# The scores of a batch's last 64 columns: four down matmuls behind the second score group, or right behind it

## Chip, cores and metric

One core of one Trainium2 chip. The metric is the device time of one execution in microseconds. Most executions of a kernel agree within 0.3%; now and then one is slower at a lower granted clock. A run more than 1.5% above the kernel's fastest counts as slow and is left out of the ratios; a milder one stays in, and is named where it matters. In all texts "position n" is the n-th of the 64 matmuls of one down stage, "the rest" is the last 64 token columns of a batch, and "a switch" is the change of PE between scores (64-row tiles) and matmuls over 128 rows. In the profile's lines PE is the matmul engine and PEld its weight loads, ACT is ScalarE, DVE is VectorE, and "<-" names what ended an idle time.

## The reference

Attention over keys and values that are averaged in groups of eight, then an up projection, `h * cos(h)`, and a down projection:

```python
k_p = k.reshape(B, H, Sp, pool, D).mean(axis=3)        # B, H, S, D = 8, 8, 576, 64; pool = 8, Sp = 72
v_p = v.reshape(B, H, Sp, pool, D).mean(axis=3)
scores = scale * np.matmul(q, k_p.transpose(0, 1, 3, 2))
attn = np.exp(scores - max); attn = attn / sum(attn)   # cut
x = np.matmul(attn, v_p) ...                           # 4608 tokens x 512
h = x @ w_in                                           # 512 -> 2048
out = (h * np.cos(h)) @ w_out                          # 2048 -> 512
```

## The kernel before

The tokens are worked in nine tiles of 512. A tile's up matmul (64 matmuls, `up_mm`) is followed by its down matmul (64, `down_mm`). A batch has 576 tokens, so tiles and batches drift apart. In tiles 1 to 6 the down matmul of tile t carries, as `fill`, the attention of batch b = t + 1: four units of 256 columns x 4 heads (`us[0]` to `us[3]`), and the rest of batch t (`REST`, 64 columns x 8 heads). A unit is scores on PE, an exp on ScalarE, values on PE, two logs and an inverse on ScalarE, two multiplies on VectorE into `xT`. All of this goes through three PSUM tiles of two banks each, called bank 0 to 2; two more single banks hold the down sums.

```python
banks = [psum.tile([128, 2, 512], FP32, name=f"bank{i}") for i in range(3)]
obanks = [psum.tile([128, 512], FP32, name=f"obank{i}") for i in range(2)]
...
def values(b, u, pair, later=None):
    ...   # matmuls into pair, two logs (L247), one inverse exp (L248) on ScalarE
    def mul():
        for hp in range(2):
            nc.vector.tensor_mul(out=x_out(b, u, half[hp]), in0=cols(pair[half[hp], hp, :], u),   # L252
                                 in1=cols(inv[half[1 - hp]], u))
...
fill = [(4, two_(0, 2, 0)), (14, V_(0, 1)), (19, V_(1, 2)), (32, two_(2, 0, 1)), (36, fill[0][1]),
        (38, V_(2, 0)), (41, V_(3, 1)), (45, fill[1][1])]
for n, (ms, fc) in enumerate(mms):
    while fi < len(fill) and fill[fi][0] <= n:
        fill[fi][1]()
        fi += 1
    down_mm(obanks[ms % 2], ms, fc)
    if fc == FFCH - 1:
        down_out(t, ms, obanks[ms % 2])
```

`V_(1, 2)` at 19 puts the values of unit 1 into bank 2. The two groups `two_` at 4 and 32 are scores of two units and then both exps. `fill[0][1]` at 36 is the rest's scores and exp, again in bank 2.

The softmax here doesn't subtract the row's maximum and nothing guards it: scores larger than these inputs give would overflow.

## Time and profile before

| | before |
|---|---|
| median of the first runs | 303.87 us |
| PE busy | 294.0 of 302.1 us |
| one steady stage (up and down of one tile) | 31.41 us |
| steady stages that the change touches | 6 |

PE is the bound: a stage is the sum of what PE has in its list, plus what PE waits. The stage length is read from one load of the cosine table to the next on ScalarE, at 115.21 and 146.62 us. The lines that carry the argument are in the prediction.

### The profile page before, as it was taken

To read this page: it belongs to the slowest core of one execution; us is meant where nothing else is said; L and a number is where in the kernel's file an instruction comes from. 1 tells how busy PE (TensorE), PEld (TensorE's weight loads), DVE (VectorE), ACT (ScalarE), POOL (GpSimd) and SP (SyncE) were. 2 spreads that over 40 slices of the span, in tenths; PEclk is the share of its full clock that TensorE was granted. 3 is DMA by queue.
4 is the path that set the end of the run, shared out by engine and by line. 5 is a ranking of instruction groups with operands and counts; after the bars stand their busy time and mean duration, and the time that the engine had idled before them with its cause. 6 is when DMAs were issued, how large, how long until landed. Compare 5 with 4: busy or idle time off the path is not lost.

```text
span 302.1 us, 4605 instructions
## 1 busy us (share of the span) xinstructions
PE 294.0 (97%) x1798; PEld 141.6 (47%) x1798; DVE 172.3 (57%) x211; ACT 206.8 (68%) x255; POOL 129.8 (43%) x92
## 2 busy tenths in 40 slices
PE   8799999999999999999999999999999999999995
PEld 3545544445544454455444544454444544444444
DVE  5558636574566366645675566656574567425712
ACT  3887897469856986688768876788578956606500
POOL 8553007984973596349733991399100000000000
PEclk9999999999999999999999999999999999999999
DMA  7999999639546943695169617881900330131032
GB/s 152 201 207 206 208 204 196 152 44 174 109 113 105 167 92 70 123 171 113 44 132 161 115 36 162 129 141 36 167 5 1 71 69 0 27 79 35 0 71 71
DMA packets 44006, 32.92 MB, mean 109 GB/s; under 512 B 22096, under 2 KB 39248, under 8 KB 43984
## 3 DMA queue, kind: packets, MB, share of 16 engines
q0 software_dynamic: 19744, 18.07, 38.2%
q1 hardware_dynamic: 24080, 14.42, 21.0%
q8 instruction: 14, 0.23, 0.3%
q10 hardware_dynamic: 160, 0.13, 0.2%
q14 instruction: 8, 0.07, 0.1%
HBM read 36.70 MB, written 9.44 MB: 153 GB/s over the span
## 4 chain that ended last, share of the span: by engine, by line
PE 85%; DMA 10%; POOL 2%; ACT 1%; issue 0%; DVE 0%; POOLq 0%; ACTq 0%
PE obank L310 39%; PE bank L297 37%; DMA w_out_sb<-in_moe_w_out_dram 6%; PE bank L241 5%; DMA w_in_sb<-in_moe_w_in_dram 4%; PE bank L211 3%; PE bank L328 1%; POOL kv_st L84 1%; POOL kp L384 1%; POOL q_b L84 1%; ACT L285 0%; ACT cos L304 0%; ACT ex L218 0%; POOL identity masks.py:197 0%; DVE o_sb L316 0%
## 5 line engine op out<-in xcount | busy, mean ns | idle before, releaser
L310 PE MATMUL obank<-w_out_sb,g_sb 128*128 128x512 bf16 x560 | 132.5, 380 | 0.5 <-DMA w_out_sb<-in_moe_w_out_dram 0.5
L297 PE MATMUL bank<-xT,w_in_sb 128*128 128x512 bf16 x576 | 126.5, 379 | 0.0
L304 ACT ACTIVATE cos<-bank,half_pi 128x1024 f32<-128x1024 f32 x72 | 80.0, 1113 | 63.3 <-PE bank L297 63.3
L307 DVE TENSOR_TENSOR g_sb<-bank,cos 128x1024 bf16<-128x1024 f32 x72 | 88.1, 1225 | 48.2 <-ACT cos L304 48.2
L297 PEld LDWEIGHTS <-w_in_sb 128*128 128x128 bf16 x576 | 55.5, 98 | 68.6 <-DVE xT L252 2.5
L310 PEld LDWEIGHTS <-g_sb 128*128 128x128 bf16 x560 | 52.2, 97 | 56.9 <-issue 3.7
L252 DVE TENSOR_TENSOR xT<-bank,inv 64x512 bf16<-64x512 f32 (+1 forms) x72 | 45.3, 629 | 50.1 <-ACT inv L248 49.2
L141 POOL TENSOR_TENSOR kv_st<-kv_st 72x2048 f32<-72x2048 bf16 x12 | 48.7, 4056 | 35.2 <-DMA kv_st<-in_k_dram 35.2
L247 ACT ACTIVATE lnc<-bank 64x512 f32<-64x512 f32 (+1 forms) x72 | 39.2, 544 | 2.9 <-PE bank L241 1.3
L218 ACT ACTIVATE ex<-bank 72x1024 bf16<-72x1024 f32 (+1 forms) x40 | 35.0, 928 | 5.3 <-PE bank L211 5.2
L316 DVE COPY o_sb<-obank 128x512 f32<-128x512 f32 x35 | 23.6, 689 | 16.8 <-PE obank L310 16.2
L142 POOL TENSOR_TENSOR kv_st<-kv_st 72x1024 f32<-72x1024 f32 x12 | 28.2, 2348 | 1.0
L248 ACT ACTIVATE inv<-lnc 128x512 f32<-128x512 f32 (+1 forms) x36 | 21.0, 583 | 1.1
L241 PE MATMUL bank<-ex,vz 72*128 72x256 bf16 (+1 forms) x176 | 20.0, 243 | 0.2 <-ACT ex L218 0.2
L241 PEld LDWEIGHTS <-vz 72*128 72x128 bf16 x176 | 13.7, 97 | 9.9 <-issue 0.6
L145 POOL TENSOR_TENSOR kp<-kv_st 72x512 bf16<-72x512 f32 x12 | 14.9, 1264 | 0.5
L211 PE MATMUL bank<-qT,kk 64*72 64x256 bf16 (+1 forms) x192 | 13.3, 252 | 1.1 <-ACT qT L193 0.5
L211 PEld LDWEIGHTS <-kk 64*72 64x72 bf16 x192 | 7.6, 110 | 11.9 <-issue 8.1
L285 ACT ACT_TABLE_LOAD x9 | 11.5, 1283 | 0.9 <-PEq L515 0.7
L288 ACT ACT_TABLE_LOAD x9 | 11.5, 1283 | 0.2
L495 POOL COPY gate<-kk 1x1 bf16<-1x1 bf16 x5 | 0.9, 180 | 24.7 <-DMA kk<-kp 24.7
L84 POOL DMA_DIRECT2D q_b<-in_q_dram x10 | 7.7, 773 | 2.7 <-DMA w_in_sb<-in_moe_w_in_dram 1.4
(55 smaller groups left out, 89.8 us busy)
## 6 DMA issues: line engine op xcount, KB each, us to landing
out_dram<-o_sb SPq DMA_DIRECT2D x70, 128.0 KB, 2.4
kv_st<-in_v_dram POOLq DMA_DIRECT2D x8, 576.0 KB, 13.0
kv_st<-in_k_dram POOLq DMA_DIRECT2D x7, 576.0 KB, 7.7
q_b<-in_q_dram POOLq DMA_DIRECT2D x6, 576.0 KB, 9.9
w_in_sb<-in_moe_w_in_dram POOLq DMA_DIRECT2D x4, 512.0 KB, 13.7
w_out_sb<-in_moe_w_out_dram POOLq DMA_DIRECT2D x4, 512.0 KB, 18.4
q_b<-in_q_dram POOLq DMA_DIRECT2D x4, 288.0 KB, 12.1
g_sb<-in_k_dram SPq DMA_DIRECT2D x1, 576.0 KB, 3.5
```

What stands on the lines that cost most here:

```text
L141: add(out=s, in0=x[:, :, 0:4, :], in1=x[:, :, 4:8, :], op=ADD)
L142: add(out=s[:, :, 0:2, :], in0=s[:, :, 0:2, :], in1=s[:, :, 2:4, :], op=ADD)
L211: nc.tensor.matmul(pair[:Sp, bank, c:c + n].rearrange("p (g n) -> p g n", n=64), lhsT=kk[b % 2][half[r], h0 + i, 0:Sp], rhs=att["qT", b][h ...
L218: nc.scalar.activation(out=ex[:, 0:nh * n].rearrange("p (a n) -> p a n", a=2), in_=pair[:Sp, :, 0:nh * n // 2], func=ACTF.Exp, scale=scale ...
L241: nc.tensor.matmul(pair[:, hp, (i // 2) * n:(i // 2 + 1) * n], lhsT=vz[b % 2][:, pj, 2 * hp:2 * hp + 2, :].rearrange("p a d -> p (a d)"), ...
L247: nc.scalar.activation(out=lnc[half[1 - hp]], in_=pair[half[1 - hp], hp, 0:w], func=ACTF.Ln)
L252: nc.vector.tensor_mul(out=x_out(b, u, half[hp]), in0=cols(pair[half[hp], hp, :], u), in1=cols(inv[half[1 - hp]], u))
L297: nc.tensor.matmul(h[:, j, :], lhsT=w_in_sb[fc // 4][:, ki, (fc % 4) * 128:(fc % 4 + 1) * 128], rhs=xT[:, ki, t * TILE:(t + 1) * TILE], st ...
L304: nc.scalar.activation(out=cos, in_=h, func=ACTF.Sin, bias=half_pi[:, :1])
L307: nc.vector.tensor_mul(out=g_sb[:, 2 * fp:2 * fp + 2, :], in0=h, in1=cos)
L310: nc.tensor.matmul(o, lhsT=g_sb[:, fc, ms * 128:(ms + 1) * 128], rhs=w_out_sb[fc // 4][:, fc % 4, :], start=(fc == 0), stop=(fc == FFCH - 1))
L316: nc.vector.tensor_copy(out=o[:, 0:n], in_=ps)
```

## The change

Its intent: the scores of the rest follow the second group's directly, so that PE switches once from down matmuls to scores and back where it switched twice; all three exps are written behind all the scores.

```diff
-            def two_(n, bank0, bank1):
+            def scores_of(*parts):
                 def go():
-                    for mm in (scores_mm, scores_exp):
-                        mm(b, us[n], banks[bank0])
-                        mm(b, us[n + 1], banks[bank1])
+                    for f in scores_mm, scores_exp:
+                        for b_, u, bank in parts:
+                            f(b_, u, banks[bank])
                 return go
-            fill = [(4, two_(0, 2, 0)), (14, V_(0, 1)), (19, V_(1, 2)), (32, two_(2, 0, 1)), (36, fill[0][1]),
+            fill = [(4, scores_of((b, us[0], 2), (b, us[1], 0))), (14, V_(0, 1)), (19, V_(1, 2)),
+                    (32, scores_of((b, us[2], 0), (b, us[3], 1), (t, REST, 2))),
                     (38, V_(2, 0)), (41, V_(3, 1)), (45, fill[1][1])]
```

## The prediction

> **What bounds the kernel now.** I read the engine totals first, then the chain that ended last, then the instructions of one steady down stage in order of time. The kernel alternates an up matmul (64 matmuls a tile) and a down matmul (64 a tile) over nine tiles; in tiles 1 to 6 the down matmul also carries the attention of the next batch, as "fill". The change touches only those six stages.
>
> Engine totals of the page (busy us, share of the span, instructions):
>
> ```profile
> PE 294.0 (97%) x1798; PEld 141.6 (47%) x1798; DVE 172.3 (57%) x211; ACT 206.8 (68%) x255; POOL 129.8 (43%) x92
> ```
>
> PE has no idle time to speak of, so whatever lengthens PE's own sequence lengthens the span. The chain that ended last says the same for a steady stage. It is merged, its columns being start us, length us, engine, tile, line, count (L310 is the down matmul, L297 the up matmul, L211 the scores, L241 the values):
>
> ```profile
> 135.95 2.81 PE obank L310 x13
> 138.76 0.56 PE bank L211 x8
> 139.31 0.97 PE obank L310 x4
> 140.28 0.26 PE bank L211 x8
> 140.54 0.54 PE obank L310 x2
> 141.07 0.44 PE bank L241 x4
> ...
> 143.70 4.10 PE obank L310 x19
> 147.80 13.90 PE bank L297 x64
> ```
>
> 13 down matmuls in 2.81 us are 0.216 us each: that is the price of one. The eight scores at 138.76 are the second score group (units 2 and 3), the eight at 140.28 are those of the batch's last 64 columns ("the rest"), and four down matmuls stand between. Exactly these four are what the change moves behind the rest.
>
> Now the same stretch with the other engines, from the timeline (start us, length us, engine, line, operation; in brackets the idle time before it and what ended it; a piece's length includes the modelled tail of its last matmul):
>
> ```profile
> 137.82 0.63 ACT L248 ACTIVATE inv<-lnc 128x512 f32<-128x512 f32 x1
> 138.02 0.69 DVE L316 COPY o_sb<-obank 128x512 f32<-128x512 f32 x1
> 138.69 0.63 PE L211 MATMUL bank<-qT,kk 64*72 64x256 bf16 x8
> 138.75 1.39 DVE L252 TENSOR_TENSOR xT<-bank,inv 64x512 bf16<-64x512 f32 x2
> 139.14 2.41 ACT L218 ACTIVATE ex<-bank 72x1024 bf16<-72x1024 f32 x3 [0.68 <-PE bank L211]
> 139.25 1.04 PE L310 MATMUL obank<-w_out_sb,g_sb 128*128 128x512 bf16 x4
> 140.21 0.21 PEld L211 LDWEIGHTS <-kk 64*72 64x72 bf16 x8 [0.42 <-DVE xT L252]
> 140.21 0.33 PE L211 MATMUL bank<-qT,kk 64*72 64x64 bf16 x8
> 140.91 0.60 PE L241 MATMUL bank<-ex,vz 72*128 72x256 bf16 x4
> 141.61 1.19 ACT L247 ACTIVATE lnc<-bank 64x512 f32<-64x512 f32 x2
> 147.72 12.20 PEld L297 LDWEIGHTS <-w_in_sb 128*128 128x128 bf16 x58 [0.41 <-DVE xT L252]
> ```
>
> The reader is to see one coincidence. The rest's scores go into bank 2. Bank 2 was last used by the values of unit 1 (position 19 of the down matmul), and VectorE's two multiplies out of it (L252) run from 138.75 to 138.75 + 1.39 = 140.14. The rest starts at 140.21, that is 0.07 us after bank 2 came free. The other five stages show the same: multiplies from 76 to 234 us of the span end 0.07 to 0.08 us before the rest's weight loads start. So position 36 was just late enough. The four down matmuls before it cover the time in which bank 2 is still being read.
>
> How quick can PE be after such a release? Tile 0 has a place where PE really was held by the same multiplies (46.42 + 1.39 = 47.81, weights at 47.86):
>
> ```profile
> 46.42 1.39 DVE L252 TENSOR_TENSOR xT<-bank,inv 64x512 bf16<-64x512 f32 x2
> 47.86 0.33 PEld L241 LDWEIGHTS <-vz 72*128 72x128 bf16 x4 [0.53 <-DVE xT L252]
> ```
>
> So 0.05 us, and the 0.07 of the steady stage leaves at most 0.02 to win.
>
> **What the Trainium skill says.** "TensorE: Matmul & The Clock Gate", section "Step-by-step: what each phase is for": matmuls stay in program order, and only weight loads are pulled ahead. So a score that waits for bank 2 holds every down matmul behind it; the trace agrees as far as it goes (the held values of tile 0 let nothing pass). The same page, "Back-to-back issue gap", gives about 216 ns for an isolated 512-column gap and 131 ns as sustained; the trace has 2.81/13 = 216 ns in a sustained stream, and I use that. "PSUM — Partial Sum Buffer", section "PSUM bank collisions raise a hardware error", says that a bank that two engines touch is not arbitrated, so software has to order them; that is the wait the rest carries, and it cannot be dropped. "Perfetto Trace Analysis", section "Tensor Engine Instruction (MATMUL, LD_WEIGHTS)", says that a matmul's reported start is its prefetch and its end an estimate; hence the tenth of a microsecond of slack in my sums.
>
> **The change part by part.** The instruction order confirms what the diff suggests. On PE, in each of the six stages, four down matmuls move from before the rest's eight scores to after them; nothing is added or removed. ScalarE's and VectorE's orders do not change at all: ScalarE ran the three exps in that same order already. "All their exps behind both" is therefore only the order in the program text.
>
> - Taken away: one switch from scores back to down matmuls. Ten down matmuls after the first score group take 2.26 us in the chain, 0.10 above 10 x 0.216, and the four here take 0.97, 0.11 above 0.864. So a switch costs about 0.1 us, up to 0.6 us for six stages, if nothing else is in the way.
> - Added: a hold. After the eight scores PE is ready for the rest at about 139.25. Bank 2 comes free at 140.14 + 0.05 = 140.19. When VectorE gets there depends on nothing that moves: last up matmul, the cos, the table load, two exps, the logs and inverses on ScalarE up to 138.45, with an output copy (138.02 to 138.71) just ahead on VectorE. PE therefore idles about 0.94 us, where it ran four down matmuls before.
> - Moved: those four, 4 x 0.216 = 0.864 us, now run after the rest. The rest starts at 140.19 in place of 140.21. Before, values of unit 2 started 0.70 us after the rest began (eight scores, two downs); now 0.70 + 0.864. They go from 140.91 to about 140.19 + 1.56 = 141.75, +0.84.
> - Does it carry to the end of the stage? ScalarE's logs started at 141.61, directly behind the exps (139.14 + 2.41 = 141.55) and behind the values. Now they wait for the values, about 142.45. From there ScalarE and then VectorE run without gaps until the multiply that the next up matmul waits for (147.72), so this shifts by the same 0.84, and so do PE's own 19 last down matmuls. PE also saves a little by starting the rest on an empty array: the down matmul's modelled tail, 139.25 + 1.04 = 140.29, reached 0.08 past the rest's start. That may give back up to 0.08 a stage.
>
> Sum: 0.76 to 0.86 us a stage, I take 0.82; times 6 is 4.9 us. On 303.87: 308.8 us, +1.6%.
>
> **The rivals.**
>
> - The switch is saved and no hold appears: 303.87 - 0.6 = about 303.3. For it speaks the intent, and that PE's weight loads were idle 0.42 us before the rest exactly as before the other score groups, where the profile names no releaser but issue, so the rest may not have been held before. Against it: no hold before says nothing of 0.9 us earlier, when the multiplies have run for only half a microsecond.
> - The hold is there but is absorbed, because ScalarE or VectorE was the bound of the second half of the stage and has slack to give. The up matmul's first weights waited for VectorE (0.41 us idle at 147.72), and steady up stages take 13.90 us where the one behind tile 0 takes 13.81, so the attention chain is level with PE, not behind it. At most 0.09 a stage comes back if the chain should move less than PE: 308.3.
> - The exps come later too: if the first exp had to wait for the rest's scores, it would start at about 140.5 in place of 139.14, the logs behind the third exp at 142.9 and not 142.45, and another 0.45 us a stage would be lost: 311.5, +2.5%. Against it: the two exps have their own matmuls to wait for, the list of waits on ScalarE is the same in both kernels, and only the third exp reads bank 2.
> - A slow restart after each idle, 0.1 to 0.2 us: 309.4 to 310.0. Nothing in tile 0's held values shows one.
>
> **Range and chances.** The floor is firm: the rest cannot be written before 140.14, so four matmuls less 0.07 and less the 0.08 tail remain, 0.71 a stage, 308.1. The ceiling of the plain mechanism is 0.86 and some latency, 309.3; a slow restart adds half a microsecond. I give 308.0 to 309.8. Two per cent is 309.95, so slower by more needs the restart or the late exps: 0.09. Faster by 2% would need 6 us that no step offers: 0.01. Within 2%: 0.90.
>
> **What would show it.** In the changed profile the rest's scores should begin about 0.05 us after the end of L252, with PE idle 0.8 to 0.95 us before them (5 us in all, put down to VectorE's xT), PE busy time unchanged or a little lower, and a stage of about 32.2 us where it was 31.4. The six down matmuls after the rest should take about 1.3 to 1.4 us, the exps should start as long after the second score group as before, and ScalarE should be idle about 0.8 us before the logs. I am wrong if L252 ends earlier in the stage than now, if the stage does not stretch although the hold is there, or if the first exp starts only after the rest.

## The result

| | before | after |
|---|---|---|
| median | 303.81 us (4 runs, 303.62 to 308.21) | 308.81 us (4 runs, 308.65 to 309.09) |
| PE busy | 294.0 us | 293.9 us |
| one steady stage | 31.41 us | 148.88 - 116.62 = 32.26 us |

The changed kernel is slower by a ratio of 1.0168, 95% interval 1.0148 to 1.0188: clear of noise, and inside 2%. Ratios here are the mean time of one kernel's fast runs over that of the other's of the same rounds, so not quite the ratio of the medians quoted. PE does the same work in the same busy time; the 5 us are waiting. Six stages of 0.85 us are 5.1 us, close to the 5.0 between the medians.

The chain that ended last in the changed kernel, over one steady stage (start us, length us, what), to be laid beside the chain of the kernel before:

```profile
140.17 0.36 PE bank L211 x4
140.53 0.02 issue
140.55 1.03 ACT ex L218
141.58 0.03 issue
141.61 0.33 PE bank L211 x8
141.94 1.40 PE obank L310 x6
143.34 0.44 PE bank L241 x4
...
145.96 4.10 PE obank L310 x19
150.06 13.91 PE bank L297 x64
```

The chain now leaves PE in mid-stage and comes back 1.08 us later. It goes through ScalarE's exp, and not through VectorE as forecast. The timeline of the same stage shows why one should not take that at its word:

```profile
138.02 1.20 ACT L247 ACTIVATE lnc<-bank 64x512 f32<-64x512 f32 x2
...
140.10 0.63 PE L211 MATMUL bank<-qT,kk 64*72 64x256 bf16 x8
140.16 1.39 DVE L252 TENSOR_TENSOR xT<-bank,inv 64x512 bf16<-64x512 f32 x2
140.55 2.41 ACT L218 ACTIVATE ex<-bank 72x1024 bf16<-72x1024 f32 x3 [0.68 <-PE bank L211]
141.61 0.21 PEld L211 LDWEIGHTS <-kk 64*72 64x72 bf16 x8 [1.14 <-DVE xT L252]
141.61 0.33 PE L211 MATMUL bank<-qT,kk 64*72 64x64 bf16 x8 [0.88 <-ACT ex L218]
143.17 0.60 PE L241 MATMUL bank<-ex,vz 72*128 72x256 bf16 x4
143.87 1.19 ACT L247 ACTIVATE lnc<-bank 64x512 f32<-64x512 f32 x2 [0.91 <-PE bank L241]
```

VectorE's multiplies end at 140.16 + 1.39 = 141.55, ScalarE's first exp of the group at 141.58, and the rest starts at 141.61. The weight load is put down to VectorE, the matmul to ScalarE. Both releases lie within 0.03 us, and the profile names the last. By what the program needs, the exp has nothing to do with the rest's scores: it reads bank 0. But a wait can be laid wider than the need, so this had to be tested.

The list of waits (us in total, times, longest), first of the kernel before, then of the changed one:

```profile
PEld L211 <- DVE xT L252: 3.0, 7, 0.4
```

```profile
PEld L211 <- DVE xT L252: 7.3, 7, 1.1
PE bank L211 <- ACT ex L218: 5.3, 6, 0.9
```

The last line is the loss: six idles of PE, 5.3 us, which the kernel before does not have.

### The profile page after: what moved, and what is told of

The parts are those of the page before. It is cut to its first block, busy times and chain, and to the rows that moved or that the text cites. A ratio compares the mean times of both kernels' runs of the same rounds, so it can differ in the third digit from the quotient of the medians.

```text
span 306.9 us, 4605 instructions
## 1 busy us (share of the span) xinstructions
PE 293.9 (96%) x1798; PEld 142.3 (46%) x1798; DVE 172.4 (56%) x211; ACT 206.8 (67%) x255; POOL 129.8 (42%) x92
## 4 chain that ended last, share of the span: by engine, by line
PE 83%; DMA 9%; ACT 3%; POOL 2%; issue 1%; DVE 0%; POOLq 0%; ACTq 0%
PE obank L310 39%; PE bank L297 36%; DMA w_out_sb<-in_moe_w_out_dram 6%; PE bank L241 5%; DMA w_in_sb<-in_moe_w_in_dram 3%; PE bank L211 3%; ACT ex L218 2%; PE bank L328 1%; POOL kv_st L84 1%; POOL kp L384 1%; POOL q_b L84 1%; ACT L285 0%; ACT cos L304 0%; POOL identity masks.py:197 0%; DVE o_sb L316 0%
```

## The experiments

Theory 1 is the prediction's: the rest's scores wait for VectorE's multiplies of unit 1 out of bank 2. Theory 2 is what the chain of the changed kernel shows: they wait for ScalarE's first exp. The first four runs shared a chip, the last two another one. One of the seven runs of the kernel before on the first chip took 307.08 us at a clock of 0.989 and still counts as fast; without it the ratios of these four runs would be about 0.0015 higher. Two of the runs below hold such a run of their own; there the medians and the steady stages say more than the ratio.

Two things could be settled without a run. A kernel that puts the two exps of the second group in the text before the rest's scores, all at position 32, builds into the same instructions with the same waits on all five engines as the changed kernel (but for the numbering of the exps' buffers). "All their exps behind both" changes nothing; the position of the rest's scores is the whole change. And the built program of the changed kernel says what the rest waits for: its first weight load waits for unit 1's second multiply on VectorE, its first matmul for unit 1's second log on ScalarE, both of which read bank 2. That log had ended at 138.02 + 1.20 = 139.22 us; no exp is in either wait. The runs have to say whether the time follows this.

**The output copy first on VectorE, in the changed kernel.** The multiplies of unit 0 are emitted two positions later, behind the copy of the first 128 output rows, which then runs in time that VectorE had idle.

```diff
-            fill = [..., (14, V_(0, 1)), (19, V_(1, 2)),
+            fill = [..., (14, V_(0, 1, later)), (16, lambda: later.pop()()), (19, V_(1, 2)),
```

> The changed kernel with VectorE's order turned: the output copy of the first 128 rows goes ahead of both units' multiplies, so the multiplies of unit 1 can start when their inverse is ready (138.45 in the profile before) and not behind the copy (138.75). Theory 1, VectorE's multiplies hold the rest's scores: bank 2 comes free about 0.28 us earlier in each of six stages, so 308.8 - 1.7 = 307.1 us, and PE's idle before the rest falls from 0.9 to about 0.6 us. Theory 2, the hold is ScalarE's first exp of the second group (the releaser that the profile after names for the matmul, it ends within 0.03 us of the multiplies): nothing on ScalarE moves, so 308.8 us as the changed kernel.

Measured: 307.66 us median (307.35 to 307.87), ratio to before 1.0108 (1.0054 to 1.0162), correct. Timeline of this kernel:

```profile
139.91 1.39 DVE L252 TENSOR_TENSOR xT<-bank,inv 64x512 bf16<-64x512 f32 x2 [0.50 <-ACT inv L248]
140.10 0.63 PE L211 MATMUL bank<-qT,kk 64*72 64x256 bf16 x8
140.56 2.42 ACT L218 ACTIVATE ex<-bank 72x1024 bf16<-72x1024 f32 x3 [0.67 <-PE bank L211]
141.36 0.33 PE L211 MATMUL bank<-qT,kk 64*72 64x64 bf16 x8 [0.63 <-DVE xT L252]
```

In both profiles the second score group starts at 140.10, so they can be laid over each other. The multiplies moved from 140.16 to 139.91, and the rest from 141.61 to 141.36: both by 0.25 us. The rest again starts 0.06 us behind the multiplies (139.91 + 1.39 = 141.30), and the profile now names VectorE. Theory 2 wanted no change; here the rest even starts before the first exp has ended (140.56 and the 1.03 us that it has in the chain of the changed kernel, 141.59). Per stage the gain is 32.26 - 32.01 = 0.25 us, 1.5 us in six, a little under the 0.28 expected. The medians show 1.13 us, taken against the kernel with the group at 29 below (308.79 us on the same chip, as slow as the changed kernel); the difference to 1.5 is of the size of the spread of the runs and is left open.

**The same turn in the kernel before, as control.** The edit is the same, made in the list before.

> The same turn of VectorE's order in the kernel before, as control. Theory 1: there the four down matmuls cover the multiplies anyway, so nothing: 303.8 us within 0.3. If the turn alone is worth time in any kernel (a shorter VectorE chain), it would be about 1.7 us here too: 302.1.

Measured: 304.06 us median (303.95 to 307.66), ratio 1.0019 (0.9943 to 1.0095), correct. The profiled run was the one of 307.66: its clock was 0.91 in the first 60 us, so nothing is read from there; its steady stage is 150.21 - 118.80 = 31.41 us, exactly that of the kernel before, although the multiplies start 0.19 us before the second score group there (142.09 and 142.28) and not 0.06 behind it. So bank 2 a quarter of a microsecond earlier is worth nothing where four down matmuls cover it, and is worth time only where PE stands waiting.

**The rest at 34.**

```diff
-                    (32, scores_of((b, us[2], 0), (b, us[3], 1), (t, REST, 2))),
+                    (32, scores_of((b, us[2], 0), (b, us[3], 1))), (34, scores_of((t, REST, 2))),
```

> The rest's scores two down matmuls behind the second group, halfway between the two kernels. Theory 1, the rest is pinned to the release of bank 2 and each down matmul ahead of it is covered: halfway, 308.8 - 6 x 2 x 0.216 = 306.2 us. If the loss were that of two neighbouring score groups of different batches (a step, not a slope), it would be gone at once: 303.8.

Measured: 306.16 us median (305.88 to 310.81, the last slow), ratio 1.0059 (0.9977 to 1.0142), correct. The steady stage is 147.40 - 115.57 = 31.83 us, halfway between 31.41 and 32.26. The loss is a slope: each down matmul taken from in front of the rest costs its own 0.216 us a stage, since the rest stays tied to the multiplies: in that profile it starts at 140.56 us, 0.06 behind their end (139.11 + 1.39).

**The second group at 29, the rest left at 32.**

```diff
-                    (32, scores_of((b, us[2], 0), (b, us[3], 1), (t, REST, 2))),
+                    (29, scores_of((b, us[2], 0), (b, us[3], 1))), (32, scores_of((t, REST, 2))),
```

> The changed kernel with the second group's scores and exps three down matmuls earlier (29), the rest left at 32. Theory 1, VectorE's multiplies hold the rest: they do not move, so the rest still starts about 0.05 us after them and the time stays, 308.5 to 309.0 us. Theory 2, ScalarE's first exp of the second group holds it: that exp starts about 0.65 us earlier, so the rest does too, and about 3.9 us come back: 304.9.

Measured: 308.79 us median (308.52 to 309.01), ratio 1.0145 (1.0092 to 1.0199), correct. Timeline of this kernel:

```profile
140.26 2.66 ACT L218 ACTIVATE ex<-bank 72x1024 bf16<-72x1024 f32 x3
140.52 1.39 DVE L252 TENSOR_TENSOR xT<-bank,inv 64x512 bf16<-64x512 f32 x2
141.97 0.33 PE L211 MATMUL bank<-qT,kk 64*72 64x64 bf16 x8 [0.77 <-DVE xT L252]
```

The exps now start before the multiplies, the first ends some 0.7 us before the rest starts (140.26 and the 1.03 that it has in the chain of the changed kernel), and still the rest waits, 0.06 us behind the multiplies' end at 141.91. The stage is 149.24 - 116.98 = 32.26 us. Theory 2 falls: moving the exp by itself moves nothing, and moving the multiplies moves the rest.

**All three at 36.** The join without the hold, to see whether the saved switch is there at all.

```diff
-                    (32, scores_of((b, us[2], 0), (b, us[3], 1), (t, REST, 2))),
+                    (36, scores_of((b, us[2], 0), (b, us[3], 1), (t, REST, 2))),
```

> All three groups of scores together, but at position 36, where bank 2 is free: the join without the hold. If PE's own sequence were all that counts: one switch of 0.1 us a stage saved, 303.8 - 0.6 = 303.2 us. My theory says that ScalarE's chain is level with PE from the second group to the stage's end: the exps start 4 x 0.216 = 0.86 us later, the logs go from 141.6 to 142.45 and the last multiply and the next up matmul with them, so about 0.8 us a stage is lost all the same, 303.8 + 4.8 = 308.6, with PE idle before the next up matmul and not before the rest's scores.

Measured: 309.78 us median (309.45 to 313.41), ratio 1.0235 (1.0176 to 1.0295; called unclear at 2%, and lifted by a run of 313.41 at a clock of 0.987 that counts as fast), correct. This is the slowest of all, and slower than expected by 1.2 us. Timeline of this kernel:

```profile
137.82 4.01 PE L310 MATMUL obank<-w_out_sb,g_sb 128*128 128x512 bf16 x17
...
140.06 0.69 DVE L316 COPY o_sb<-obank 128x512 f32<-128x512 f32 x1
...
140.81 0.53 PEld L310 LDWEIGHTS <-g_sb 128*128 128x128 bf16 x3 [0.29 <-issue]
...
142.22 2.41 ACT L218 ACTIVATE ex<-bank 72x1024 bf16<-72x1024 f32 x3 [1.72 <-PE bank L211]
...
150.77 2.55 PE L297 MATMUL bank<-xT,w_in_sb 128*128 128x512 bf16 x11 [0.59 <-DVE xT L252]
```

The expected part is there: ScalarE waits 1.72 us for the second group where it waited 0.68, all its work up to the stage's end starts later, and PE idles at the next up matmul (0.59 us, and 0.19 before the values of unit 2) and not before the rest. The term that I had not seen is the copy at 140.06. The first down matmul of the third row block, at position 32, reuses the down bank that this copy empties until 140.75; the built program has that wait, though the profile names only "issue". In the kernel before, the second score group stands in front of it and covers the copy; here it comes right behind 13 matmuls that end at about 137.82 + 13 x 0.216 = 140.63, and starts at about 140.81, a loss of some 0.17 us. A stage is 149.66 - 117.24 = 32.42 us: 1.01 more than before, of which 0.86 are the later exps.

**The rest with the first group, at 9, the banks turned.** Here the join is made where three banks are free. The price is that the later scores and the values of all units go into other banks, the first group moves from 4 to 9, and the values of unit 2 from 38 to 37.

```diff
-            fill = [(4, scores_of((b, us[0], 2), (b, us[1], 0))), (14, V_(0, 1)), (19, V_(1, 2)),
-                    (32, scores_of((b, us[2], 0), (b, us[3], 1), (t, REST, 2))),
-                    (38, V_(2, 0)), (41, V_(3, 1)), (45, fill[1][1])]
+            fill = [(9, scores_of((b, us[0], 2), (b, us[1], 0), (t, REST, 1))), (14, V_(0, 2)), (19, V_(1, 0)),
+                    (32, scores_of((b, us[2], 1), (b, us[3], 2))),
+                    (37, V_(2, 1)), (41, V_(3, 2)), (45, lambda: values(t, REST, banks[0]))]
```

> The join made where a bank is free: the rest's scores with the first group, at position 9, into bank 1, with the banks of the later units turned so that none of the waits is on a bank still read. ScalarE is idle 0.68 us before the second group's exps in the kernel before, and the rest's exp (0.55 us) now goes ahead of that. My theory: one switch (0.1 us) and the 0.09 us by which the up matmul waited for the last multiply are saved in each of six stages: 303.8 - 1.1 = 302.7 us. Rivals: no gain because a switch costs nothing (303.3 to 303.8), or a loss of 0.5 us a stage because the logs of the first units start later (306.8).

Measured: 302.54 us median of 5 (302.38 to 302.80), ratio 0.9963 (0.9950 to 0.9976), correct. It is the fastest kernel, by 0.4% over the kernel before. Its chain over one stage:

```profile
131.88 0.84 PE bank L211 x16
132.72 1.19 PE obank L310 x5
...
138.67 0.56 PE bank L211 x8
...
147.36 13.81 PE bank L297 x64
```

Sixteen scores in one go take 0.84 us, 0.02 more than 0.56 and 0.26 apart, but the surcharge on the down matmuls behind scores (1.19 for five, 0.11 above 5 x 0.216) is paid twice a stage and no longer three times. And the up matmul takes 13.81 and not 13.90 us, since the attention chain now ends before PE needs it (the last multiply at 147.04 us, the last down matmul at about 147.20). The two together are 0.2 us less the 0.02 by which the joined scores are longer; the stage is 146.01 - 114.78 = 31.23, 0.18 less than before. So the gain that the change was after exists, at some 0.1 us a stage. No run has the saved switch alone; the split is read from the chain.

## Why the prediction was right

- **The hold.** Forecast: the rest would be pinned to the end of VectorE's multiplies, PE idle about 0.94 us. Measured: six idles of 0.88 us (the profile counts from the modelled end of the scores, 140.10 + 0.63; counted as forecast, from 0.56 us behind their start, it is 0.95). The rest is 0.06 us behind the multiplies; it moves with them (copy first) and not with the exp (group at 29). Counted from the start of the second group, the rest starts at 1.51 us where it was at 1.52.
- **The four matmuls behind it.** Forecast: the values of unit 2 go back by 0.84 us. Measured from the start of the second group: 143.17 - 140.10 = 3.07 against 140.91 - 138.69 = 2.22, so 0.85. The run with the rest at 34 shows the price of each.
- **Does it reach the stage's end.** Forecast yes, ScalarE waiting about 0.8 us before its logs. Measured: 0.91 us of wait there, the stage longer by 0.85. (The prediction's own times, 142.45 less 141.55, give 0.90, and not the 0.8 that it names.)
- **The saved switch.** Priced at 0.1 us a stage if nothing else is in the way, and left out of the sum; the last run shows that it is real, and the changed kernel that it does not come through.
- **The empty array.** This term, up to 0.08 us a stage given back, was wrong: nothing came back. From the rest's start to the down matmuls behind it is 0.26 us in both kernels (140.21 to 140.47, 141.61 to 141.87). The rest and the six down matmuls took 0.33 + 1.40 us in the chain, with the 0.1 surcharge of a switch. The Trainium skill, "TensorEngine Tiling (Array Packing)", section "Key Properties", says that a change of tiling mode drains the engine; then the rest met an empty array before as well. The trace fits that: the weight loads of all score groups in the steady stages of the kernel before follow 0.42 us of idle. The sum was so 0.85 and not 0.82 a stage, 5.1 and not 4.9 us, inside the range. That the median met the forecast to 0.01 us is in part luck: the first of the six stages came 0.27 us sooner in the changed kernel's profile (table loads at 50.17 and 50.44 us).
- **The rivals.** Exps that wait for the rest: no, the first exp starts 0.45 us behind the second group's start in both kernels. A slow restart: no, 0.06 us. Slack on ScalarE or VectorE that absorbs the hold: no; all three at 36 shows that this side is as tight as PE.

What the prediction did not foresee was which engine the profile would name for the hold: VectorE, as forecast, for the weight load, but ScalarE for the matmul.

## What to carry to other kernels

Before work is moved ahead, look at what its buffer's last reader is doing at the new place: work that stands in front of a wait may be what hides it, even where the profile shows hardly any wait, and on an engine that works in order one held instruction costs all that it used to follow. If a join is worth something, make it where a buffer is free, and check the engine fed by it as well. Where two releases fall within a few hundredths of a microsecond, the named releaser is a guess; read the waits of the built program, and move each by itself.

## What the Trainium skill lacked or had wrong

- "TensorE: Matmul & The Clock Gate", section "Back-to-back issue gap": its sustained 131 ns for a 512-column matmul with its own weight load is not what runs here; 13 in a row take 2.81 us, 216 ns each, the figure that this section gives for an isolated gap. The same page, section "Step-by-step: what each phase is for", has 215.7 ns for 512 columns back to back; that figure agrees with the trace.
- "TensorEngine Tiling (Array Packing)", section "Key Properties", names the drain at a change of tiling mode but no cost. A drain is not seen as such in the trace; here down matmuls behind 64-row scores take about 0.11 us more than their count times 0.216, and removing one such place together with a 0.09 us wait gave 0.18 us a stage.
- No page among those read gives the time from a VectorE release to PE's start: 0.05 to 0.06 us here, also where PE had been idle for 0.88 us.
- "Perfetto Trace Analysis", section "Optimization Strategy", advises finding the semaphore that a gap waits on and who updates it; it does not warn that where two releases lie 0.03 us apart (141.55 and 141.58) the engine that a view names can be the wrong one: here ScalarE's exp, which the built program does not wait for.
